# Range tests of the rounded weights: where they write, when they are issued, and where two roundings stand in their turns

## The chip, the core and the metric

The kernel runs on one core of one Trainium2 chip. The metric is the device time of one execution in microseconds (us). Before the change the median of three runs was 1049.61 us (1048.46 to 1050.42). The profiled execution had a span of 1047.8 us in the profile and 1049.67 us as a timed run.

A core has five engines that run their own instruction streams side by side: PE (matrix multiply), DVE (vector), ACT (activation functions), POOL (a second elementwise engine) and SP, which here only issues transfers. PEld stands for the weight loads of PE. Within one engine the instructions start in the order in which the program issues them.

## The reference, cut to what matters

```python
# q, k, v: (4, 8, 768, 64)   centroids: (8, 16, 64)
q_assign = argmax(q_n @ c_n), k_assign = argmax(k_n @ c_n)   # cluster of each row
scores = where(q_assign == k_assign, q @ k.T / 8, -1e9)
attn = softmax(scores);  y = attn @ v
x = y as (3072, 512)                      # (B*S, H*D)
h = x @ w_in                              # w_in (512, 2048)
out = (h * sigmoid(1.702 * h)) @ w_out    # w_out (2048, 512)
```

`w_in` and `w_out` arrive as 64-bit floats, which the kernel reads as pairs of 32-bit words and turns into 32-bit floats itself. That step is called rounding below.

## The kernel before, in words

`fast` does the whole computation under assumptions on the range of its data. It gathers evidence for these assumptions in a tile `row_sums`, and if a test at the end fails, a second function (`general`) computes everything again.

**Attention.** The 32 heads are handled as 16 pairs (`p`), four per batch. Queries are taken in halves of 384, so there are 32 groups `g` of one pair and one half, and each group has six units `u` (one tile of 128 keys each). The main loop (line 608) takes two units per **turn** `t`, with 96 turns and two more to drain. In a turn, in the order of issue: the scores of two units (PE, L397, and for the first four pairs a second product `part`, L411, that carries the cluster mask); their exponentials (ACT, L422); a weight rounding, if the table `pace` has one; the range test of the last softmax denominators (`check`, ACT, L481 and L483); the mask and the running sum (DVE L433 from turn 24 on, POOL L443); near scores of a later pair (`prep_near`, PE L289, copied by ACT L295); the values of the turn before (PE L454); every third turn a normalisation (PE L466, DVE reciprocal L469 and multiply L471); preparation of later pairs (transposes L275 with their copies L280 on ACT, cluster choice L300 to L321, one-hot copies L362 with L367 on DVE and L369 on ACT); chunks of the feed-forward part (PE L520 or L500, then ACT L490 and DVE L491); and a second rounding, in turns from 14 on.

Three PSUM banks named `m` serve the transposes, near scores, normalisation, feed-forward chunks and, in turns 5 to 13, the rounding. A PE instruction that needs a bank waits until the ACT or DVE instruction that reads the bank's previous content has ended.

**Rounding of the weights.** The weights are 32 chunks of 128x512 (0 to 15 are `w_in`, 16 to 31 `w_out`; chunk 31 is `w_out[:, 15, :]`). `load_w` fetches a chunk's pairs of words into one of three buffers `raw` (SP, 512 KB). `round_next(i)` takes chunk `i`: it issues the load of chunk `i + 2`, then four DVE operations (L177, L180, L182, L185; L177 and L180 read the high words, L185 the low words) and one addition L187, on DVE in turns 0 to 13 and on POOL from turn 14. Before the change chunks 0 to 7 belong to turns 0, 2, 5, 8, 9, 11, 12 and 13, and from turn 14 each turn has two: chunk 8 + 2(t - 14) in the middle (after the exponentials) and the next at the end. Turn 25 has chunks 30 and 31. In turn 13 the rounding stands at the end.

**Range test of a chunk.** `check_w` (L191) is two ACT operations, L197 (square) and L199 (exp), each with a sum along the row into `row_sums`. It is issued at the head of the *next* rounding, and it writes its elementwise result, which nobody uses, over the high words that it reads. So L197 waits until DVE's L180 of that chunk has read them. The load of chunk `i + 2` reuses the buffer of chunk `i - 1`, and so waits for L185 of that chunk and for its test.

`manual_schedule` keeps the order of issue as it is written. Before the change the test of chunk 0 stands in turn 2, that of chunk 1 in turn 5, that of chunk 31 in turn 26.

**After attention** (its last scores start at 587 us, the next product, L740, at 602 us) the rest of the feed-forward part follows, which the change does not touch.

Of the kernel before, what the change touches and what calls it, by code (L numbers as in the profile page):

```python
# [8 lines left out]
FP32 = mybir.dt.float32  # L9
# [4 lines left out]
AF = mybir.ActivationFunctionType  # L14
# [24 lines left out]
def fast(  # L39
# [26 lines left out]
    nc = tc.nc  # L66
# [11 lines left out]
    NF = DF // P  # L78
# [28 lines left out]
    def bank():  # L107
        return ps_m.tile([P, 512], FP32, name="m")
# [17 lines left out]
    def load_v(p):  # L126
# [16 lines left out]
    w_chunks = [  # L143
        (w[:, c, n:n + WN],
         src.bitcast(I32)[c * P:(c + 1) * P, 2 * n:2 * (n + WN)])
        for w, src, n_c, n_n in ((w_in, moe_w_in, NCH, DF),
                                 (w_out, moe_w_out, NF, DM))
        for n in range(0, n_n, WN) for c in range(n_c)]
    NW = len(w_chunks)
    w_raw, w_pow = {}, {}  # L150

    def load_w(i):
        if i < NW:
            t = wp.tile([P, WN, 2], I32, name="raw")
            nc.sync.dma_start(out=t.rearrange("p n t -> p (n t)"),
                              in_=w_chunks[i][1])
            w_raw[i] = t
# [2 lines left out]

    ODD = -2 ** 30
    POWER = -2 ** 23
    w_done, w_read = [0], {}

    def round_next(in_psum=False, engine=nc.gpsimd):

        i = w_done[0]
        if i - 1 in w_read:
            check_w(i - 1)
        if i == NW:  # L170
            return
        load_w(i + 2)
        raw, w = w_raw.pop(i), w_chunks[i][0]
        e = wp.tile([P, WN], I32, name="e", bufs=2)
        a = bank() if in_psum else w
        hi, lo, a_i = raw[:, :, 1], raw.bitcast(U32)[:, :, 0], a.bitcast(I32)
        nc.vector.tensor_scalar(out=a_i, in0=hi, scalar1=3, scalar2=0x3FFFFFF8,  # L177
                                op0=ALU.logical_shift_left,
                                op1=ALU.bitwise_and)
        nc.vector.scalar_tensor_tensor(out=a_i, in0=hi, scalar=ODD, in1=a_i,  # L180
                                       op0=ALU.bitwise_and, op1=ALU.bitwise_or)
        nc.vector.tensor_scalar(out=e, in0=a_i, scalar1=POWER, scalar2=None,  # L182
                                op0=ALU.bitwise_and)
        e = e.bitcast(FP32)
        nc.vector.scalar_tensor_tensor(out=e, in0=lo, scalar=2.0 ** -52, in1=e,  # L185
                                       op0=ALU.mult, op1=ALU.mult)
        engine.tensor_tensor(out=w, in0=a, in1=e, op=ALU.add)  # L187
        w_read[i] = raw
        w_done[0] += 1

    def check_w(i):  # L191

        y = w_read.pop(i).bitcast(FP32)[:, :, 1]
        nc.scalar.activation(out=y, in_=y, func=AF.Square,  # L197
                             accum_out=row_sums[:, 2, i:i + 1])
        nc.scalar.activation(out=y, in_=y, func=AF.Exp, scale=-2.0 ** 12,  # L199
                             bias=fifteen[:, 0:1],  # L200
                             accum_out=row_sums[:, 3, i:i + 1])

    def round_to(n):
        while w_done[0] < n:
            round_next()
# [51 lines left out]
    for a in range(2):  # L257
        rows = slice(a * D, (a + 1) * D)
        nc.vector.tensor_copy(
            out=cT[rows, :, a, :],  # L260
            in_=cps[rows, 0:P].rearrange("d (h a c) -> d h a c", a=2,
                                         c=NC)[:, :, a, :])
# [128 lines left out]
    def scores(u):  # L391
        g, kt = divmod(u, NJ)
        p, h = split(g)
        ps = ps_s.tile([P, 2, 512], FP32, name="s")
        for a in range(2):
            rows = slice(a * D, (a + 1) * D)
            nc.tensor.matmul(out=ps[:, a, 0:HALF],  # L397
                             lhsT=T[p, 1][rows, kt * P:(kt + 1) * P],
                             rhs=T[p, 0][rows, h * HALF:(h + 1) * HALF],
                             start=True, stop=(p >= HP))  # L400
        s_of[u] = ps[:, :, 0:HALF]

    def part(u):

        g, kt = divmod(u, NJ)
        p, h = split(g)
        if p >= HP:
            return
        for a in range(2):
            r = 32 * (2 * (p % 2) + a)  # L410
            nc.tensor.matmul(  # L411
                out=s_of[u][:, a, :],
                lhsT=hots[p // 2, 1][r:r + NC, kt * P:(kt + 1) * P],
                rhs=hots[p // 2, 0][r:r + NC, h * HALF:(h + 1) * HALF],
                start=False, stop=True)

    def exps(u):
        p, h = split(u // NJ)
        s = s_of[u]
        if p < HP:  # L420
            A_of[u] = ap.tile([P, 2, HALF], FP32, name="A")
        nc.scalar.activation(out=A_of[u] if p < HP else s, in_=s, func=AF.Exp,  # L422
                             scale=SCALE)

    def mask(u):

        g, kt = divmod(u, NJ)
        p, h = split(g)
        s = s_of.pop(u)
        if p >= HP:  # L430
            A_of[u] = ap.tile([P, 2, HALF], FP32, name="A")
            for a in range(2):
                nc.vector.scalar_tensor_tensor(  # L433
                    out=A_of[u][:, a, :],
                    in0=qcode[p][:, a, h * HALF:(h + 1) * HALF],
                    scalar=code[p][:, kt % NH, 1, kt // NH, a:a + 1],
                    in1=s[:, a, :], op0=ALU.is_equal, op1=ALU.mult)
        A = A_of[u]
        if kt == 0:
            return  # L440
        if kt == 1:
            sum_of[g] = ap.tile([P, 2, HALF], FP32, name="sum", bufs=2)
        nc.gpsimd.tensor_tensor(out=sum_of[g],  # L443
                                in0=A_of[u - 1] if kt == 1 else sum_of[g],
                                in1=A, op=ALU.add)
# [31 lines left out]
    def check(g):  # L477


        rec = recs.pop(g)  # L480
        nc.scalar.activation(out=rec, in_=rec, func=AF.Copy,  # L481
                             accum_out=row_sums[:, 0, g:g + 1])
        nc.scalar.activation(out=rec, in_=rec, func=AF.Relu, bias=top[:, 0:1],  # L483
                             scale=-2.0 * LIMIT * LIMIT,
                             accum_out=row_sums[:, 1, g:g + 1])
# [22 lines left out]
    half_ffn, ffn = deque(), deque()  # L508
# [63 lines left out]
    NT = NU // 2  # L572
    TG = NJ // 2
    TB = 2 * HP * TG

    prep_at = {}
    for p in range(1, NPAIR):
        b, hp = divmod(p, HP)
        for i in range(2 if p == 1 else 0, len(PREP)):
            if p == 1:  # L580
                t = (i - 2) // 2
            elif b == 0:
                t = (hp - 2) * TG + 1 + i // 2
            else:
                t = b * TB + TG * hp - (7, 7, 6, 6, 4, 3, 2)[i]
# [5 lines left out]
    def prep(p, i):  # L591
        if i == 0 and p:
            load_v(p)
        PREP[i](p)
        if i in (1, 3) and loads:
            load_qk(*loads.popleft())

    rate = 1.6


    pace = {t: 1 for t in (0, 2, 5, 8, 9, 11, 12, 13)}
    pace.update((t, 2) for t in range(TB // 2 + 2, NT))
    owed = 0.0
# [4 lines left out]
    for t in range(NT + 2):  # L608
        us = range(2 * t, 2 * t + 2) if t < NT else ()
        for u in us:  # L610
            scores(u)
        if t == 0:
            prep(0, 6)
        for u in us:
            part(u)
        for u in us:
            exps(u)
        second_half = t >= TB // 2
        how = ((False, nc.gpsimd) if t >= TB // 2 + 2 else
               (t > 2, nc.vector))  # L620
        if pace.get(t) and t != TB // 2 + 1:
            round_next(*how)
        if recs:
            check(*recs)
        for u in us:
            mask(u)
        work = sorted(prep_at.get(t, ()), key=lambda w: PREP[w[1]] != prep_near)
        while work and PREP[work[0][1]] == prep_near:
            prep(*work.pop(0))
        if 1 <= t <= NT:  # L630
            for u in range(2 * t - 2, 2 * t):
                values(u)

        kept = NF // 2 if t < NT - 3 else NF // 4
        todo = half_ffn or (ffn if len(ffn) > kept else ())
        owed += (rate if half_ffn else 0.65 if kept > NF // 4 else 1.0) if todo else -owed
        g = (t - 2) // TG if t >= 2 and (t - 2) % TG == TG - 1 else None
        if g is not None and second_half:
            normalise(g)
        for p, i in work:  # L640
            prep(p, i)
        if g is not None and not second_half:
            normalise(g)
        while owed >= 1 and todo:
            todo.popleft()()
            owed -= 1
        if pace.get(t) == 2 or t == TB // 2 + 1:
            round_next(*how)
    check(*recs)
    qcode.clear()  # L650
# [649 lines left out]
```

## Time and profile before

| what | value |
|---|---|
| median of three runs | 1049.61 us |
| span of the profiled execution | 1047.8 us |
| PE busy, 0 to 228 us / 228 to 1048 us | 192.2 us / 804.9 us |
| DVE busy, 88 to 148 us | 55.2 us of 60 |
| idle of ACT before L197, ended by DVE's L180 | 20.8 us in 11 waits |
| load of one weight chunk, issue to landing (min, median, max) | 3.5, 4.0, 6.0 us |

The page of a profile gives busy times and a strip of 40 slices, each with a digit for its busy share in tenths. The row PEclk in that strip is the clock that PE was granted. The answers on waits give the engine and line that stood idle, the engine and line whose end released it, and total us, number and longest. A row of the timeline has the start, the duration, the engine, the line, the operation and its tiles, and in brackets the idle time of that engine just before and its releaser. The rounding and its tests lie in the first 220 us. All turns up to 26 lie there: turn 2's exponentials start at 25.68, turn 3's at 37.06, turn 14's at 88.15, turn 20's at 144.03, turn 21's at 161.85, turn 25's at 205.47 and turn 26's at 216.27.

### The profile page before, as it was taken

To read this page: it belongs to the slowest core of one execution; us is meant where nothing else is said; L and a number is where in the kernel's file an instruction comes from. 1 tells how busy PE (TensorE), PEld (TensorE's weight loads), DVE (VectorE), ACT (ScalarE), POOL (GpSimd) and SP (SyncE) were. 2 spreads that over 40 slices of the span, in tenths; PEclk is the share of its full clock that TensorE was granted. 3 is DMA by queue.
4 is the path that set the end of the run, shared out by engine and by line. 5 is a ranking of instruction groups with operands and counts; after the bars stand their busy time and mean duration, and the time that the engine had idled before them with its cause. 6 is when DMAs were issued, how large, how long until landed. Compare 5 with 4: busy or idle time off the path is not lost.

```text
span 1047.8 us, 12571 instructions
## 1 busy us (share of the span) xinstructions
PE 997.1 (95%) x4574; PEld 583.0 (56%) x4574; DVE 677.4 (65%) x1055; ACT 374.2 (36%) x761; POOL 418.8 (40%) x304
## 2 busy tenths in 40 slices
PE   7799778889999999999999999999999999999997
PEld 3334334334455345544455355688755788655886
DVE  4679887764577867776877577743477634576431
ACT  4567554642355545555554322200022200222000
POOL 2565654443466556655666767600022100120000
PEclk9999888999999999999999999999999999999999
DMA  7323443520002310131000000000000000000000
GB/s 219 79 71 119 132 146 96 153 63 18 19 17 61 91 39 19 31 83 40 26 1 1 1 11 0 1 21 21 21 0 1 1 21 21 21 0 1 21 21 23
DMA packets 66118, 45.25 MB, mean 43 GB/s; under 512 B 52096, under 2 KB 60032, under 8 KB 66048
## 3 DMA queue, kind: packets, MB, share of 16 engines
q1 hardware_dynamic: 65904, 44.33, 14.7%
q8 instruction: 38, 0.62, 0.2%
q14 instruction: 32, 0.26, 0.1%
q10 hardware_dynamic: 144, 0.03, 0.0%
HBM read 38.04 MB, written 6.31 MB: 42 GB/s over the span
## 4 chain that ended last, share of the span: by engine, by line
PE 83%; DVE 10%; ACT 4%; issue 1%; DMA 0%; POOL 0%; SPq 0%; DVEq 0%; ACTq 0%; POOLq 0%
PE b L797 21%; PE b L740 21%; PE s L397 11%; PE o L454 10%; PE m L500 7%; PE m L549 4%; PE m L520 3%; PE m L275 2%; PE m L466 2%; DVE short L469 1%; DVE e L185 1%; DVE w_in L180 1%; PE m L289 1%; DVE w_out L180 1%; DVE A L433 1%
## 5 line engine op out<-in xcount | busy, mean ns | idle before, releaser
L443 POOL TENSOR_TENSOR sum<-sum,A 128x768 f32<-128x768 f32 x128 | 235.2, 1837 | 135.0 <-DVE A L433 114.3
L433 DVE SCALAR_TENSOR_TENSOR A<-qb,code,s 128x384 f32<-128x384 uint8 x288 | 157.4, 607 | 86.3 <-ACT s L422 51.3
L397 PE MATMUL s<-T,T 64*128 64x384 f32 x768 | 155.6, 519 | 2.5 <-DVE A L433 0.6
L454 PE MATMUL o<-A,inv 128*64 128x384 f32 x768 | 146.0, 502 | 1.1 <-ACT x L459 1.1
L422 ACT ACTIVATE s<-s 128x768 f32<-128x768 f32 x144 | 108.8, 793 | 103.1 <-PE s L397 90.8
L731 DVE TENSOR_TENSOR G<-b,G 128x384 f32<-128x384 f32 x168 | 93.3, 555 | 48.5 <-PE b L740 41.6
L678 POOL TENSOR_TENSOR W<-w_in 128x256 f32<-128x256 f32 x24 | 17.7, 738 | 261.2 <-PE b L740 259.4
L490 ACT ACTIVATE th<-G 128x384 f32<-128x384 f32 x96 | 50.2, 523 | 163.5 <-DVE G L731 103.1
L397 PEld LDWEIGHTS s<-T,T 64*128 64x128 f32 x768 | 66.1, 188 | 76.0 <-issue 35.0
L731 DVE TENSOR_TENSOR y<-b,y 128x256 f32<-128x256 f32 x54 | 22.1, 422 | 130.1 <-PE b L797 93.8
L740 PE MATMUL b<-x,w_in 128*128 128x384 f32 x288 | 101.2, 486 | 0.0
L454 PEld LDWEIGHTS o<-A,inv 128*64 128x64 f32 x768 | 46.9, 137 | 86.3 <-issue 82.5
L469 DVE RECIPROCAL short<-m 128x384 f32<-128x384 f32 x32 | 81.6, 2551 | 7.3 <-PE m L466 7.1
L443 POOL TENSOR_TENSOR sum<-A 128x768 f32<-128x768 f32 x32 | 58.4, 1826 | 67.4 <-DVE A L433 32.3
L491 DVE SCALAR_TENSOR_TENSOR G<-th,G 128x384 f32<-128x384 f32 x96 | 68.5, 713 | 16.8 <-ACT th L490 14.2
L740 PEld LDWEIGHTS b<-x,w_in 128*128 128x128 f32 x288 | 54.7, 190 | 37.9 <-issue 0.5
L740 PE MATMUL b<-x,W 128*128 128x384 f32 x192 | 71.0, 493 | 0.0
L797 PE MATMUL b<-Z,G 128*128 128x256 f32 x288 | 65.1, 379 | 0.0
L797 PE MATMUL b<-w_out,G 128*128 128x256 f32 x288 | 63.6, 379 | 0.0
L520 PE MATMUL m<-x,w_in 128*128 128x384 f32 x128 | 50.7, 552 | 11.8 <-ACT short L295 6.8
L500 PE MATMUL m<-w_out,g 128*128 128x512 f32 x120 | 59.1, 611 | 2.3 <-ACT T L280 2.3
L797 PEld LDWEIGHTS b<-w_out,G 128*128 128x128 f32 x288 | 54.6, 190 | 8.0
(122 smaller groups left out, 1339.2 us busy)
## 6 DMA issues: line engine op xcount, KB each, us to landing
raw<-in_moe_w_in_dram SPq DMA_DIRECT2D x16, 512.0 KB, 4.2
raw<-in_moe_w_out_dram SPq DMA_DIRECT2D x16, 512.0 KB, 3.5
in<-in_q_dram SPq DMA_DIRECT2D x32, 192.0 KB, 4.2
in<-in_k_dram SPq DMA_DIRECT2D x32, 192.0 KB, 3.2
inv<-in_v_dram SPq DMA_DIRECT2D x16, 384.0 KB, 4.0
out_dram<-y SPq DMA_DIRECT2D x15, 256.0 KB, 2.4
qb<-line SPq DMA_DIRECT2D x12, 192.0 KB, 3.3
out_dram<-y SPq DMA_DIRECT2D x18, 128.0 KB, 1.8
```

What stands on the lines that cost most here:

```text
L397: nc.tensor.matmul(out=ps[:, a, 0:HALF], lhsT=T[p, 1][rows, kt * P:(kt + 1) * P], rhs=T[p, 0][rows, h * HALF:(h + 1) * HALF], start=True, ...
L422: nc.scalar.activation(out=A_of[u] if p < HP else s, in_=s, func=AF.Exp, scale=SCALE)
L433: nc.vector.scalar_tensor_tensor(out=A_of[u][:, a, :], in0=qcode[p][:, a, h * HALF:(h + 1) * HALF], scalar=code[p][:, kt % NH, 1, kt // NH ...
L443: nc.gpsimd.tensor_tensor(out=sum_of[g], in0=A_of[u - 1] if kt == 1 else sum_of[g], in1=A, op=ALU.add)
L454: nc.tensor.matmul(out=o_of[g][a * D:(a + 1) * D, 0:HALF], lhsT=v_in[p][:, a, kt, :], rhs=A[:, a, :], start=(kt == 0), stop=(kt == NJ - 1))
L469: nc.vector.reciprocal(out=rec, in_=ps[:, 0:HALF])
L491: nc.vector.scalar_tensor_tensor(out=g, in0=t, scalar=1.0, in1=h, op0=ALU.add, op1=ALU.mult)
L500: nc.tensor.matmul(out=ps[:, 0:DM], lhsT=g, rhs=w_out[:, f, :], start=(f == 0), stop=(f == NF - 1))
L520: nc.tensor.matmul(out=ps[:, 0:HALF], lhsT=w_in[:, c, f * P:(f + 1) * P], rhs=xT[c], start=(c == 0), stop=(c == NCH - 1))
L731: nc.vector.tensor_tensor(out=o, in0=p, in1=a, op=ALU.add)
L740: nc.tensor.matmul(out=ps[:, 0:HALF], lhsT=a[:, c], rhs=x(c), start=(c == 0), stop=(c == 1))
L797: nc.tensor.matmul(out=ps[:, 0:DN], lhsT=a(f // 4)[:, f % 4], rhs=z(f), start=(f == 0), stop=(f == FB - 1))
```

## The change

Four things change. The test of chunk `i` is issued right after the rounding of the same chunk, where before it stood ahead of the next one. Its elementwise result goes to the place of chunk 31 in `w_out`, which is empty until chunk 31 itself is rounded; only the test of chunk 31 still writes over its own high words. The roundings of turns 0 and 2 are issued at the end of their turns. And the line that counts feed-forward chunks (`owed`) is written out in branches with the same values.

```diff
     def round_next(in_psum=False, engine=nc.gpsimd):
         i = w_done[0]
-        if i - 1 in w_read:
-            check_w(i - 1)
         if i == NW:
             return
         load_w(i + 2)
...
         engine.tensor_tensor(out=w, in0=a, in1=e, op=ALU.add)
-        w_read[i] = raw
+        check_w(i, raw, w_chunks[NW - 1][0] if i < NW - 1 else raw.bitcast(
+            FP32)[:, :, 1])
         w_done[0] += 1
-    def check_w(i):
-        y = w_read.pop(i).bitcast(FP32)[:, :, 1]
-        nc.scalar.activation(out=y, in_=y, func=AF.Square,
+    def check_w(i, raw, z):
+        nc.scalar.activation(out=z, in_=raw.bitcast(FP32)[:, :, 1],
+                             func=AF.Square,
                              accum_out=row_sums[:, 2, i:i + 1])
-        nc.scalar.activation(out=y, in_=y, func=AF.Exp, scale=-2.0 ** 12,
+        nc.scalar.activation(out=z, in_=z, func=AF.Exp, scale=-2.0 ** 12,
                              bias=fifteen[:, 0:1],
                              accum_out=row_sums[:, 3, i:i + 1])
...
-        if pace.get(t) and t != TB // 2 + 1:
+        late = t <= 2 or t == TB // 2 + 1
+        if pace.get(t) and not late:
             round_next(*how)
...
-        if pace.get(t) == 2 or t == TB // 2 + 1:
+        if pace.get(t) == 2 or pace.get(t) and late:
             round_next(*how)
```

No instruction is added or removed on any engine. In the built program the order on DVE differs in one place (in turn 2, L367 comes ahead of the rounding of chunk 1), on ACT each test stands one place earlier (that of chunk 31 at the end of turn 25), and on SP the loads of chunks 2 and 3 come after a pair of q loads.

More of the change, by code (lines that the diff above doesn't have):

```diff
@@ L162, in fast @@
     POWER = -2 ** 23
-    w_done, w_read = [0], {}
+    w_done = [0]
     def round_next(in_psum=False, engine=nc.gpsimd):
         i = w_done[0]
-        if i - 1 in w_read:
-            check_w(i - 1)
         if i == NW:
@@ L635, in fast @@
         todo = half_ffn or (ffn if len(ffn) > kept else ())
-        owed += (rate if half_ffn else 0.65 if kept > NF // 4 else 1.0) if todo else -owed
+        if not todo:
+            owed = 0.0
+        elif half_ffn:
+            owed += rate
+        else:
+            owed += 0.65 if t < NT - 3 else 1.0
         g = (t - 2) // TG if t >= 2 and (t - 2) % TG == TG - 1 else None
```

## The prediction

> **What bounds the kernel now.** I first read the page's busy times and clock strip, to see where PE, the busiest engine, loses time.
>
> ```profile
> PE 997.1 (95%) x4574; PEld 583.0 (56%) x4574; DVE 677.4 (65%) x1055; ACT 374.2 (36%) x761; POOL 418.8 (40%) x304
> PEclk9999888999999999999999999999999999999999
> ```
>
> PE lacks 50.7 us of the span. By windows, 35.8 of them lie before 228 us (192.2 busy), and there the clock drops too. The change touches nothing later, so only this stretch can gain, and from 228 us on PE is full (40.00 of 40 us in 248 to 288), so what is won or lost before should reach the end one to one. Next come the waits, which name what PE and ACT stood still for.
>
> ```profile
> PE m L520 <- ACT short L295: 6.8, 2, 5.0
> PE m L275 <- DVE qb L367: 4.7, 1, 4.7
> PE m L275 <- ACT short L295: 2.7, 1, 2.7
> ACT raw L197 <- DVE w_in L180: 12.1, 6, 4.4
> ACT raw L197 <- DVE w_out L180: 7.4, 4, 3.9
> ACT raw L197 <- DVE m L180: 1.3, 1, 1.3
> ```
>
> The last three are the 20.8 us in which ACT waits for a rounding to read its words. Whether they cost anything depends on what stands behind them, so I read the timeline at the three long waits of PE: in turn 2,
>
> ```profile
> 26.77 2.24 DVE L180 SCALAR_TENSOR_TENSOR w_in<-raw,w_in 128x512 int32<-128x512 int32 x1
> 29.05 1.91 DVE L182 TENSOR_SCALAR e<-w_in 128x512 int32<-128x512 int32 x1
> 32.44 0.56 DVE L367 COPY qb<-m 64x768 bf16<-64x768 bf16 x1
> 33.06 0.61 PE L275 MATMUL m<-ident,in 128*128 128x128 f32 x3 [4.73 <-DVE qb L367]
> ```
>
> in turns 20 and 21,
>
> ```profile
> 149.39 0.67 ACT L197 ACTIVATE raw<-raw 128x512 f32<-128x512 f32 x1 [3.87 <-DVE w_out L180]
> 152.69 7.19 PE L520 MATMUL m<-x,w_in 128*128 128x384 f32 x16 [4.96 <-ACT short L295]
> 155.18 3.70 POOL L443 TENSOR_TENSOR sum<-sum,A 128x768 f32<-128x768 f32 x2
> 167.81 5.46 PE L520 MATMUL m<-x,w_in 128*128 128x384 f32 x8 [3.43 <-DVE short L309]
> ```
>
> and in turns 25 and 26.
>
> ```profile
> 216.27 1.50 ACT L422 ACTIVATE s<-s 128x768 f32<-128x768 f32 x2 [3.44 <-PE s L397]
> 218.18 0.69 DVE L180 SCALAR_TENSOR_TENSOR w_out<-raw,w_out 128x512 int32<-128x512 int32 x1
> 218.91 0.69 ACT L197 ACTIVATE raw<-raw 128x512 f32<-128x512 f32 x1 [1.15 <-DVE w_out L180]
> 221.72 0.46 ACT L295 COPY short<-m 128x384 f32<-128x384 f32 x1
> 222.23 0.55 PE L275 MATMUL m<-ident,in 128*128 128x128 f32 x3 [2.67 <-ACT short L295]
> ```
>
> The reader should see: in turn 2 a whole rounding of 6.1 us stands ahead of a 0.56 us copy that PE needs; in turn 20 ACT's wait for DVE is passed on to PE through L295; in turn 25 the last chunk's L180 ends only at 218.87, after the exponentials of turn 26 have begun.
>
> **What the skill says.** (1) "TensorE: Matmul & The Clock Gate", Part 1: PE's clock is halved after an idle window of about 3.4 us and restored after a busy one, and the windows run free of the program. The trace agrees: after the 4.96 us wait sixteen L520 take 7.19 us, where sixteen elsewhere take 5.43, with a clock of 0.50 in 150 to 156 us; but idle times from 2.1 us (at 52 us) already halved it, and one of 2.67 us did not. (2) "SBUF — State Buffer", section Who interferes with whom: a DVE instruction with two inputs in SBUF, or in a two-port mode, and a GpSimd (POOL) instruction that reads SBUF exclude each other for the whole instruction. The trace agrees: L180 takes 0.69 us alone and 2.24 beside POOL's sums. (3) The same TensorE page, section on the 32x32 array: ACT and DVE are strict first in, first out. So a test that waits holds everything behind it; L295 at 152.18 shows it.
>
> **The change, part by part.**
>
> *Turn 2: the rounding of chunk 1 moves behind L367 (DVE), its L197/L199 to the end of the turn (ACT), the load of chunk 3 behind two q loads (SP).* The one-hot transposes start at 27.02; at 43.01 the same copy starts 0.53 us after them, so L367 would run at 27.55 to 28.11. PE's first three transposes end at 28.34, so the 4.73 us wait goes to nothing. The scores behind it took 2.93 us at the halved clock, against 1.56 usually: 1.4 more. On ACT, L369 no longer stands behind the test of chunk 0, so the copies L280 end about 29.6; then comes chunk 1's test, 1.65 us, and the exponentials of turn 3 at 31.25 where PE would allow 30.95. Before they start at 37.06: **gain 5.8**. Bounds: 6.1 without the test in the way; 4.3 if the moved rounding, which now meets POOL's sums of both turns, holds up L306 of turn 3 (free until 34.05 by my count, rounding done about 33.1) by one sum less its margin, 1.5. I take 5.8. Chunk 3's load isn't needed before turn 8; SP gives its place to q loads that wait for PE.
>
> *Turn 0: the same move.* On DVE no other instruction changes places with it. On ACT the test of chunk 0 falls into 18.25 to 19.9, inside the 2.10 us that ACT idles before 20.34. The load of chunk 2 goes from 14.52 to about 18.6, needed at 48.87. Nothing, hidden by those.
>
> *Turns 14 to 19: waits of L197.* Seven of the eleven waits lie here, 13.4 us. DVE is 55.2 us busy of 60 in 88 to 148, and PE waits for it (L469, L491), not for ACT. ACT would run ahead of DVE and wait for loads instead: a load now follows L185 of the chunk three before, plus 4.0 us; chunk 14's would land about 114.4 where ACT comes by about 112.4. Where PE gains 0.4 us (turn 17), the DVE work behind it then waits for POOL's L443. Nothing, hidden by DVE; at most 1.
>
> *Turn 20.* Chunk 20's load lands about 144, so its test starts at 145.5, when the exponentials end, instead of 149.39. From L197 to L295 it is 2.79 us, so L295 starts at 148.3 and L520 at 148.8: 3.9 earlier, and with 1.1 us idle the clock stays up (1.76). PE ends sixteen L520 at 154.3, 5.6 earlier. But the next rounding on DVE then falls from 155.4 into POOL's L443 (155.18 to 158.88). Its two last operations (0.43 and 0.69) come after that: done at about 160.4, before at 163.31. The next rounding and L306, L309 follow unbroken, and L520 of turn 21 waits for L309: 165.0 instead of 167.81. **Gain 2.8**; bounds 0 and 5.6 (no loss to POOL, or all of it).
>
> *Turns 25 and 26: the test of chunk 31.* It is the one that still writes over its words, and now stands at the end of turn 25, ahead of the exponentials of turn 26. A wait is added: ACT is held from about 209.7 until L180 ends at 218.87. Behind it: both L422 of turn 26, L481, L483, L295, L280; for these wait DVE's masks, and PE's L275. The test takes 1.57, so the exponentials start at 220.5 instead of 216.27. The test no longer stands behind them, so L295 starts at 223.2 instead of 221.72: 1.5 later. PE then idles 4.2 us instead of 2.67, which by the cases above should halve the clock for one window, 1.7 of work. **Loss 3.2**; bounds 1.5 (clock stays up) and 4.9 (two windows, as in 115 to 122 us).
>
> Sum: -5.8 - 2.8 + 3.2 = **-5.4** on the span of 1047.8. That execution was timed at 1049.67, beside a median of 1049.61, so I take the median: **1044.2 us**.
>
> **The rivals.** (a) *POOL takes all of turn 20's gain*: -5.8 + 3.2 = -2.6, 1047.0. For it: DVE is the bound there, and three of the four rounding operations have been seen stretched to about 2 us; against it: DVE idles 3.98 and 2.03 us in that stretch. (b) *The last test costs nothing*, as DVE comes to it earlier or PE finds other work: -8.6, 1041.0. For it: PE has two matmul groups ready (L454, L397); against it: they end before 219.6. (c) *The waits are only replaced*: in turn 2 L369 or a load takes L367's place and ACT waits for loads elsewhere, so the change doesn't do what it says: 1049.6. Against it: L369 would end at 28.7, long before 33. (d) *Slower: the held ACT queue of turn 25.* If all 10.8 us from 209.7 to 220.5 came onto the path instead of their tail, the sum would be -8.6 + 10.8 = +2.2: 1051.8. It decides from 8.6. Against it: before, too, ACT starts nothing of turn 26 until 216.27, as PE's scores come only then.
>
> **How the numbers follow.** Forecast 0.50, (a) 0.20, (b) 0.18, (c) 0.06, (d) 0.06. About 0.2%, 2.1 us, is what a measurement of this kernel can tell from no change, so faster means below 1047.5. Case (a) lies 0.5 us inside that; I give it 0.14 of faster and 0.06 of same. Faster 0.50 + 0.18 + 0.14 = 0.82, same 0.06 + 0.06 = 0.12, slower 0.06. The range goes down past (b) by the open 1.5 of turns 2 and 20, to 1039.5, and up past (a) by 1.0 of clock windows, to 1048.0; (c) and (d), 0.12, stay out.
>
> **What would show it.** Right: PE's wait for L367 gone and turn 3's exponentials 5 to 6 us earlier; no L197 released by L180 except one, of about 9 us, before turn 26; PE's wait for L295 near 149 down to about 1 us; a longer one for L309 near 159 (5 to 6 us) and for L295 near 215 (about 4 us). Wrong: L197 waits for loads by many us, or PE's wait near 215 grows with the whole hold.

## The result, and the profile after

The changed kernel takes 1042.84 us (median of four runs, 1041.59 to 1044.41), beside 1049.03 us for the kernel before: ratio 0.9941, 95% interval 0.9922 to 0.9959. Run again beside other kernels (7 below) it took 1042.45 us (1041.06 to 1042.99), ratio 0.9915 (0.9892 to 0.9937). It is faster: by 6.2 us in the first comparison and by 10.0 in the second, where the kernel before had a median of 1052.42 us. The prediction was a gain of 5.4 us, to 1044.2. The profiled execution has a span of 1040.6 us, where the one of before had 1047.8. From here on, lines 196 and 199 are the range test that stood at L197 and L199; the rounding is now L175, L178, L180, L183 and L185.

The page of the changed kernel, busy times and clock strip:

```profile
PE 993.8 (96%) x4574; PEld 583.8 (56%) x4574; DVE 681.7 (66%) x1055; ACT 372.8 (36%) x761; POOL 418.6 (40%) x304
PEclk9999898999999999999999999999999999999999
```

PE lacks 46.8 us of the span, against 50.7 before. Half of the 7.2 us, then, is idle time that is gone; the rest is PE busy time, 997.1 to 993.8: the same matmuls at a higher clock. What PE waited for in the first 230 us, and what ACT waited for before the tests (line, releaser, total us, number, longest):

```profile
PE m L520 <- DVE short L309: 5.2, 1, 5.2
PE m L275 <- ACT short L295: 4.1, 1, 4.1
PE m L520 <- DVE x L491: 2.8, 2, 2.1
PE m L520 <- ACT short L295: 2.4, 2, 1.7
```

```profile
ACT raw L196 <- DVE w_out L178: 10.3, 1, 10.3
...
ACT w_out L196 <- DMA raw<-in_moe_w_in_dram: 6.7, 3, 2.6
```

The 4.7 us for L367 are gone from PE's list. The 6.8 us for L295 before L520 are 2.4. Three waits have grown: L309 from 3.4 to 5.2, L295 before L275 from 2.7 to 4.1, and L491 before L520 from 1.1 to 2.8 (its longest from 0.6 to 2.1, in turn 16). On ACT the eleven waits for the rounding are one, of 10.3 us; three waits for loads have come in their place.

Where the time went is read by laying the starts of ACT's exponentials (L422) of chosen turns side by side. "Again" is the profile of the changed kernel's second measurement.

| stretch | before, us | changed | again | predicted difference | measured, changed / again |
|---|---|---|---|---|---|
| start to turn 2 | 25.68 | 25.30 | 26.04 | 0 | -0.4 / +0.4 |
| turn 2 to 3 | 11.38 | 5.32 | 5.30 | -5.8 | -6.1 / -6.1 |
| turn 3 to 7 | 23.06 | 21.12 | 22.67 | 0 | -1.9 / -0.4 |
| turn 7 to 14 | 28.03 | 28.18 | 28.19 | 0 | +0.2 / +0.2 |
| turn 14 to 20 | 55.88 | 56.33 | 57.53 | 0, at most 1 | +0.5 / +1.7 |
| turn 20 to 22 | 31.23 | 28.87 | 27.33 | -2.8 | -2.4 / -3.9 |
| turn 22 to 25 | 30.21 | 30.00 | 29.98 | 0 | -0.2 / -0.2 |
| turn 25 to 27 | 21.64 | 24.81 | 24.61 | +3.2 | +3.2 / +3.0 |
| turn 27 to the end | 820.7 | 820.7 | 819.1 | 0 | 0 / -1.6 |
| span | 1047.8 | 1040.6 | 1040.7 | -5.4 | -7.2 / -7.1 |

Two executions of the same kernel agree on the span, and differ by 1.2 to 1.6 us in four of the stretches. That is the clock, as shown below.

Turn 2 in the timeline of the changed kernel (start, duration, engine, line, in brackets the idle time before):

```profile
27.17 0.56 DVE L367 COPY qb<-m 64x768 bf16<-64x768 bf16 x1 [1.15 <-PE m L362]
...
28.38 2.19 DVE L178 SCALAR_TENSOR_TENSOR w_in<-raw,w_in 128x512 int32<-128x512 int32 x1
29.08 0.69 ACT L196 ACTIVATE w_out<-raw 128x512 f32<-128x512 f32 x1
...
30.62 1.49 ACT L422 ACTIVATE A<-s 128x768 f32<-128x768 f32 x2
```

The copy now runs ahead of the rounding. The rounding's slow operation, stretched to 2.19 us beside POOL's sum, lies behind it and holds nobody. The test starts at 29.08, though its own L178 runs until 30.57: it writes into `w_out` and follows its load alone.

Turns 20 and 21:

```profile
141.59 7.12 PE L520 MATMUL m<-x,w_in 128*128 128x384 f32 x16 [0.74 <-ACT short L295]
...
150.44 2.19 DVE L178 SCALAR_TENSOR_TENSOR w_out<-raw,w_out 128x512 int32<-128x512 int32 x1
...
157.65 0.56 DVE L309 TENSOR_TENSOR short<-m,best 128x384 bf16<-128x384 f32 x1
...
158.36 4.83 PE L520 MATMUL m<-x,w_in 128*128 128x384 f32 x8 [5.16 <-DVE short L309]
```

PE's wait just ahead of turn 20's L520 is 0.74 us, where it was 4.96. The wait that follows, for DVE's L309 in turn 21, is longer instead.

Turns 25 and 26:

```profile
207.90 0.69 DVE L178 SCALAR_TENSOR_TENSOR w_out<-raw,w_out 128x512 int32<-128x512 int32 x1
208.63 0.69 ACT L196 ACTIVATE raw<-raw 128x512 f32<-128x512 f32 x1 [10.34 <-DVE w_out L178]
...
210.18 1.48 ACT L422 ACTIVATE s<-s 128x768 f32<-128x768 f32 x2
...
212.84 0.46 ACT L295 COPY short<-m 128x384 f32<-128x384 f32 x1
...
213.35 0.70 PE L275 MATMUL m<-ident,in 128*128 128x128 f32 x3 [4.14 <-ACT short L295]
213.85 1.92 PE L500 MATMUL m<-w_out,g 128*128 128x512 f32 x2
```

ACT stands 10.34 us before the last test, with the exponentials of turn 26 behind it. PE stands 4.14 us, and L500 then runs at half clock: 1.92 us, where 1.02 is usual.

### The profile page after: what moved, and what is told of

Read it like the earlier page. It is cut to its first block, busy times and chain, and to the rows that moved or that the text cites. A ratio compares the mean times of both kernels' runs of the same rounds, so it can differ in the third digit from the quotient of the medians.

```text
span 1040.6 us, 12560 instructions
## 1 busy us (share of the span) xinstructions
PE 993.8 (96%) x4574; PEld 583.8 (56%) x4574; DVE 681.7 (66%) x1055; ACT 372.8 (36%) x761; POOL 418.6 (40%) x304
## 4 chain that ended last, share of the span: by engine, by line
PE 83%; DVE 13%; ACT 2%; issue 1%; DMA 0%; POOL 0%; DVEq 0%; ACTq 0%
PE b L803 21%; PE b L746 21%; PE s L397 11%; PE o L454 10%; PE m L500 7%; PE m L549 4%; PE m L520 3%; PE m L275 2%; DVE short L469 2%; DVE e L183 2%; PE m L466 2%; DVE w_out L178 1%; DVE e L180 1%; DVE A L433 1%; DVE w_in L178 1%
## 5 line engine op out<-in xcount | busy, mean ns | idle before, releaser
L454 PE MATMUL o<-A,inv 128*64 128x384 f32 x768 | 145.1, 499 | 1.0 <-ACT x L459 1.0
L422 ACT ACTIVATE s<-s 128x768 f32<-128x768 f32 x144 | 109.0, 793 | 99.5 <-PE s L397 87.1
L454 PEld LDWEIGHTS o<-A,inv 128*64 128x64 f32 x768 | 46.6, 136 | 85.1 <-issue 81.4
L491 DVE SCALAR_TENSOR_TENSOR G<-th,G 128x384 f32<-128x384 f32 x96 | 68.6, 714 | 16.8 <-ACT th L490 14.2
L500 PE MATMUL m<-w_out,g 128*128 128x512 f32 x120 | 60.0, 619 | 2.2 <-ACT T L280 2.2
L520 PE MATMUL m<-x,w_in 128*128 128x384 f32 x128 | 49.3, 542 | 10.3 <-DVE short L309 5.2
```

Of the source, the lines that this page charges most:

```text
L454: nc.tensor.matmul(out=o_of[g][a * D:(a + 1) * D, 0:HALF], lhsT=v_in[p][:, a, kt, :], rhs=A[:, a, :], start=(kt == 0), stop=(kt == NJ - 1))
L491: nc.vector.scalar_tensor_tensor(out=g, in0=t, scalar=1.0, in1=h, op0=ALU.add, op1=ALU.mult)
L500: nc.tensor.matmul(out=ps[:, 0:DM], lhsT=g, rhs=w_out[:, f, :], start=(f == 0), stop=(f == NF - 1))
L520: nc.tensor.matmul(out=ps[:, 0:HALF], lhsT=w_in[:, c, f * P:(f + 1) * P], rhs=xT[c], start=(c == 0), stop=(c == NCH - 1))
```

## The experiments

Two sets of four kernels, each set on one chip. The median of before was 1050.91 us (1048.12 to 1054.23, 19 runs) beside the first set and 1052.42 us (1047.86 to 1054.40, 11 runs) beside the second. The ratios are to before. Its runs spread over 6.1 and 6.5 us, with granted clocks from 0.979 to 0.984, and its one profiled execution (timed at 1049.67 us) lies in the faster half of both sets. So the differences of medians come out larger here than those between the profiles; what the slower runs of before lose, and where, no trace here shows.

| kernel | median, us (range) | ratio, 95% interval | profiled span, us |
|---|---|---|---|
| 1 the move alone | 1041.37 (1040.54 to 1042.43) | 0.9902, 0.9883 to 0.9921 | 1040.6 |
| 2 the tests alone | 1050.86 (1048.81 to 1051.59) | 0.9991, 0.9978 to 1.0003 | 1049.1 |
| 3 last test in a tile of its own | 1035.16 (1034.19 to 1035.50) | 0.9844, 0.9826 to 0.9863 | 1032.4 |
| 4 last test later | 1039.53 (1039.01 to 1042.50) | 0.9893, 0.9874 to 0.9912 | 1037.6 |
| 5 no POOL sum in turn 20 | 1040.81 (one run) | none | 1039.0 |
| 6 as 3, turn 21's rounding late | 1033.48 (1031.11 to 1034.22) | 0.9828, 0.9803 to 0.9854 | 1031.6 |
| 7 the changed kernel again | 1042.45 (1041.06 to 1042.99) | 0.9915, 0.9892 to 0.9937 | 1040.7 |
| 8 kernel 3 again | 1036.15 (1035.31 to 1037.30) | 0.9857, 0.9832 to 0.9881 | 1035.4 |

### 1 and 2: the two halves of the change

Kernel 1 is the kernel before with only the roundings moved; kernel 2 is the changed kernel with only that undone.

```diff
# 1, from the kernel before
-        if pace.get(t) and t != TB // 2 + 1:
+        late = t <= 2 or t == TB // 2 + 1
+        if pace.get(t) and not late:
...
-        if pace.get(t) == 2 or t == TB // 2 + 1:
+        if pace.get(t) == 2 or pace.get(t) and late:
# 2, from the changed kernel
-        late = t <= 2 or t == TB // 2 + 1
+        late = t == TB // 2 + 1
```

> The kernel before with one part of the change: the roundings of turns 0 and 2 stand at the end of their turns; every range test stays where it was before. My theory: the whole gain of turn 2 is this move. The exponentials of turn 3 start about 6.1 us earlier than before, counted from those of turn 2, and the time is 5 to 7.5 us below the kernel before (about 6, ratio 0.994; 1.6 us either way hang on whether a clock window of PE falls into the wait of turn 5). Rival: the tests carry the gain, and the move alone gives under 2 us.

> The changed kernel with the roundings of turns 0 and 2 back in the middle of their turns; the tests follow the loads as in the change. My theory: turns 14 to 22 give 2 to 3 us, the last test takes 3.2 back, so the time is within 2 us of the kernel before (ratio 0.999 to 1.001), with a wait of about 10 us of ACT before the last test. Rival: the tests carry the gain, and this version alone is 4 us or more faster.

In kernel 1 turn 2 to 3 took 5.37 us, 6.0 less than before; turn 20 to 22 took 31.88, no less than before's 31.23; turn 25 to 27 took 20.40, without the loss. (Turn 3 to 7 is 1.9 shorter here too, and 22 to 25 1.7 longer.) PE's waits in 138 to 178 us still show before's wait for L295 in full:

```profile
PE m L520 <- ACT short L295: 4.9, 1, 4.9
PE m L520 <- DVE short L309: 3.4, 1, 3.4
```

Kernel 2, timeline of turn 2:

```profile
32.22 0.56 DVE L367 COPY qb<-m 64x768 bf16<-64x768 bf16 x1
...
32.84 0.90 PE L275 MATMUL m<-ident,in 128*128 128x128 f32 x3 [4.72 <-DVE qb L367]
```

From turn 7 on its stretches are those of the changed kernel: turn 20 to 22 28.88 us (-2.4), turn 25 to 27 24.81 (+3.2).

So the move alone gives the gain of the whole change: kernel 1 and the changed kernel have the same profiled span, and the interval of its ratio overlaps that of kernel 7 (they did not run side by side). Kernel 1's median is 9.5 us below that of before, more than the 5 to 7.5 expected, while its span is 7.2 below: the profiled execution of before was 1.2 us faster than the median there, and that of kernel 1 1.1 slower. The tests by themselves can't be told from no change, because their gain in turn 20 is spent again in turn 25, along with the small losses of turns 3 to 20 (+0.8 together).

### 3 and 4: the last test

```diff
# 3, from the changed kernel
-        check_w(i, raw, w_chunks[NW - 1][0] if i < NW - 1 else raw.bitcast(
-            FP32)[:, :, 1])
+        check_w(i, raw, w_chunks[NW - 1][0] if i < NW - 1 else yp.tile(
+            [P, DM], FP32, name="y"))
# 4, from the changed kernel: chunk 31's test, in place, in the middle of turn 26
...
+        if i < NW - 1:
+            check_w(i, raw, w_chunks[NW - 1][0])
+        else:
+            w_read[i] = raw
...
```

> The changed kernel, but the test of chunk 31 writes its elementwise result into the output tile y, which nothing uses before turn 26, so it too follows its load alone. My theory: ACT's wait of 10.3 us before the last test goes, the exponentials of turn 26 start 4.2 us earlier, PE's wait for L295 near 213 falls from 4.1 us to under 0.5 and its clock stays up: 4 to 6 us below the changed kernel, about 1037.5. Rival: the wait is hidden by other work and the version is within 1 us of the changed kernel.

> The changed kernel, but the test of chunk 31 stands where it stood before the change, in the middle of turn 26, and writes over its own words. My theory: the exponentials of turn 26 start 4.2 us earlier than in the changed kernel, but the test then stands behind them and holds L295: PE waits about 2.7 us as before the change, with its clock up. About 3 us below the changed kernel, near 1040, between the changed kernel and the version with the free last test. Rival: the place of the last test does not matter, within 1 us of the changed kernel.

Kernel 3, timeline around turns 25 and 26:

```profile
197.29 0.68 ACT L196 ACTIVATE y<-raw 128x512 f32<-128x512 f32 x1
...
205.00 1.50 ACT L422 ACTIVATE s<-s 128x768 f32<-128x768 f32 x2 [6.09 <-PE s L397]
...
206.99 0.69 DVE L178 SCALAR_TENSOR_TENSOR w_out<-raw,w_out 128x512 int32<-128x512 int32 x1
```

The test of chunk 31 runs 9.7 us ahead of the L178 that it used to wait for, and the exponentials of turn 26 wait for PE's scores alone. Turn 25 to 27 takes 19.10 us: 5.7 less than in the changed kernel, and 2.5 less than before. Kernel 4 (its lines stand 5 further down: L427 exponentials, L201 test, L300 copy, L280 transposes):

```profile
206.07 1.50 ACT L427 ACTIVATE s<-s 128x768 f32<-128x768 f32 x2 [7.62 <-PE s L402]
...
208.77 0.69 ACT L201 ACTIVATE raw<-raw 128x512 f32<-128x512 f32 x1 [1.21 <-DVE w_out L181]
...
212.09 0.55 PE L280 MATMUL m<-ident,in 128*128 128x128 f32 x3 [2.73 <-ACT short L300]
```

Turn 25 to 27 takes 21.69 us there, as before (21.64), with before's wait of 2.7 us. The place of this one test is thus worth 3.1 us. Freed, at the end of turn 25, it gains another 2.6; no run splits these between the wait (1.21 us) and the test's own length (about 1.5 us), which both stand ahead of L295 in kernel 4. Kernel 3 is faster than the kernels before and after the change: 6.3 us below the changed kernel beside which it was run (8 against 7), where 4 to 6 were expected at first. It is also 6.2 us below kernel 1, so the tests, once the last one is freed too, are worth that much on top of the move.

### 5: does POOL's sum take the rest of turn 20's gain?

The kernel leaves the units of turn 20 (40 and 41) out of POOL's running sum, so that two terms are missing from it.

```diff
-        if kt == 0:
+        if kt == 0 or u in (40, 41):
```

> The changed kernel without POOL's running sum (L443) of the two units of turn 20, so two terms are missing from that sum. It asks whether this sum is what takes the rest of turn 20's gain: in the changed kernel the next rounding's L178 takes 2.19 us beside it at 150.44 and PE waits 5.16 us for L309 near 158.4. If POOL's sum is the cause, that L178 takes about 0.7 us, L309 ends 1.5 to 2 us earlier against turn 20's exponentials, PE's wait for it falls to about 3.5 us, and turn 22's exponentials start about 27.0 us after turn 20's instead of 28.9. Rival: DVE's own queue is the cause whatever POOL does; then the distance stays within 0.5 us of 28.9.

```profile
149.73 0.69 DVE L178 SCALAR_TENSOR_TENSOR w_out<-raw,w_out 128x512 int32<-128x512 int32 x1
...
155.46 0.56 DVE L309 TENSOR_TENSOR short<-m,best 128x384 bf16<-128x384 f32 x1
...
156.16 5.46 PE L520 MATMUL m<-x,w_in 128*128 128x384 f32 x8 [3.42 <-DVE short L309]
```

L178 takes 0.69 us, and the wait for L309 is 3.42. The execution to compare it with is kernel 7, in which, as here, turn 20's L520 ran at full clock. There POOL's sum stretches two operations of the rounding (L175 to 2.08 us from 0.42, L178 to 2.20 from 0.69, 3.2 together), and the wait is 6.58: 3.2 longer. In the changed kernel's first profile L178 alone is stretched by much, and the wait is 5.16: 1.7 longer. So POOL's sum is what lengthens this wait. Turn 20 to 22 takes 25.56 us, 1.8 less than kernel 7's 27.33 (1.9 was expected, counted from the changed kernel); the rest of the 3.2 went to the clock, since turn 21's eight L520 took 5.46 us here and 4.22 there. Nor did the 1.8 last: in turn 24 the same wait of 1.71 us for L280 cost half clock here (two and six L500 in 1.88 and 3.73 us, against 1.13 and 2.74 in kernel 7), which took 1.7 back.

### 6: one rounding fewer ahead of L309

```diff
# from kernel 3
-        late = t <= 2 or t == TB // 2 + 1
+        late = t <= 2 or t in (TB // 2 + 1, 21)
...
-        if pace.get(t) == 2 or pace.get(t) and late:
+        for _ in range(pace.get(t, 0) - (not late)):
             round_next(*how)
```

> The kernel with the last test in a tile of its own, and with both roundings of turn 21 at that turn's end. In that kernel PE waits 6.3 us for L309, which stands on DVE behind the rounding in the middle of turn 21. Theory (the wait is for a DVE queue with one rounding too many ahead of L309): the wait falls to about 3 us, turn 22's exponentials start 3 to 4 us earlier, and the time is 3 to 5 us below that of the kernel without this edit (about 1031 to 1032 where that one gives 1035). Rival (DVE bounds turns 20 to 25 as a whole): the two roundings in a row hold the masks and copies of turn 22, the gain is given back by turn 25, and the time is within 1 us of the kernel without this edit.

```profile
155.85 2.85 PE L520 MATMUL m<-x,w_in 128*128 128x384 f32 x8 [0.24 <-ACT T L280]
156.20 0.55 DVE L306 TENSOR_REDUCE best<-m 128x24 f32<-128x384 f32 x1
156.78 0.56 DVE L309 TENSOR_TENSOR short<-m,best 128x384 bf16<-128x384 f32 x1
```

L306 starts 17.61 us after turn 20's exponentials, against 20.84 in kernel 8: 3.2 sooner, the length of one rounding, as expected. But PE's wait went from 5.14 us to 0.24, by more than that, and L520 starts before L309 at all. The built program tells why. In kernel 3 this L520 writes the bank `m` that L309 reads; in kernel 6 the pool of these banks gave it the bank of the first transposes L275, which ACT's L280 frees. So the wait for DVE is gone altogether, and the 3.2 us alone would have left about the 3 us expected. Against kernel 8 (both with turn 20's L520 at 7.12 us) turn 20 to 22 takes 23.72 instead of 28.85 us, in part by the clock (turn 21's eight L520 in 2.85 us instead of 4.80); turn 25 to 27 gives 1.6 back, and 3.9 remain by turn 28. The medians differ by 2.7, a little under the 3 to 5 expected; the spans by 3.8. Kernel 6 is the fastest of all, 9.0 us below the changed kernel on that chip.

### 7 and 8: the same kernels again

> The changed kernel as it is, beside the others on one chip, so that they can be compared with it. It should repeat its time of about 1042.8 us, ratio 0.994 to the kernel before, and its steps: turn 3's exponentials at about 30.6 us, 28.9 us from turn 20's exponentials to turn 22's, 24.8 from turn 25's to turn 27's. If the 1.6 us between turns 6 and 7 is a matter of where a clock window falls, it may be missing here; if it is part of the change, it is there again.

> The kernel with the last test in a tile of its own, again, beside the other three. It should give about 1035 us, 6 to 8 below the changed kernel on the same chip: 5.7 from turns 25 to 27 and, if the 1.6 us near 590 us is more than chance, that too. If that was a clock window that fell well by chance, the difference may be near 6.

Kernel 8 stands 6.3 us below kernel 7, within the expected 6 to 8. Kernel 7 repeats the time, but not the ratio, since the kernel before was slower beside it. It repeats the steps of turns 2 and 25, but not those of turns 3 to 7, of 14 to 22 and of the end. Turns 5 and 6, the changed kernel and then kernel 7:

```profile
47.11 0.85 PE L289 MATMUL m<-T,cT 128*32 128x384 f32 x8 [2.08 <-DVE w_in L185]
47.89 1.51 PE L454 MATMUL o<-A,inv 128*64 128x384 f32 x8
```

```profile
47.85 1.50 PE L289 MATMUL m<-T,cT 128*32 128x384 f32 x8 [2.08 <-DVE w_in L185]
49.28 2.39 PE L454 MATMUL o<-A,inv 128*64 128x384 f32 x8
```

After attention, in the same order:

```profile
599.49 1.65 PE L746 MATMUL b<-T,W 128*128 128x384 f32 x2 [2.55 <-DVE T L684]
600.93 2.35 PE L746 MATMUL b<-x,W 128*128 128x384 f32 x4
```

```profile
601.24 0.91 PE L746 MATMUL b<-T,W 128*128 128x384 f32 x2 [2.55 <-DVE T L684]
601.99 1.45 PE L746 MATMUL b<-x,W 128*128 128x384 f32 x4
```

The same wait, to the hundredth, is followed by full clock in one execution and by half clock in the other: 1.5 to 1.6 us each time. In the kernel before both fell badly (L289 1.51, L454 2.48, and 809.2 us from turn 28 to the end, as in the changed kernel; 807.6 in kernel 7). So the 1.6 us between turns 6 and 7 belong to no part of the change. Nor do those after attention that kernel 3 seemed to have gained: kernels 6, 7 and 8 have them too.

## Why the prediction was right, step by step

**Turn 2, -5.8 predicted, -6.1 measured.** The copy L367 was placed at 27.55 us; with the 0.38 us by which the changed kernel reached turn 2 sooner, it started at 27.55. The test began 0.1 sooner than expected and took 1.5 us instead of 1.65. Kernels 1 and 2 show that this step is the move alone.

**Turn 0 and turns 14 to 19, 0 predicted, or at most 1.** Turn 0 is below what the start tells: two executions lie 0.4 on either side. In turns 14 to 19 ACT did turn from waiting for DVE to waiting for loads, as written (6.7 us in three waits). That DVE hides the gain is true of the sum: in the changed kernel turns 14 and 15 are 2.4 us shorter than before, and turns 16 and 17 give 2.9 back. In turn 16 PE now waits 2.1 us for DVE's L491, where before had 0.52 and kernel 1 0.55. The stretch grew by 0.3 and 0.5 us in kernel 2 and the changed kernel, and by 1.7 in kernel 7, which is beyond the bound of 1. That excess is the clock. After nearly the same wait the changed kernel and then kernel 7 show

```profile
99.06 2.85 PE L520 MATMUL m<-x,w_in 128*128 128x384 f32 x8 [2.13 <-DVE x L491]
```

```profile
101.29 4.54 PE L520 MATMUL m<-x,w_in 128*128 128x384 f32 x8 [2.09 <-DVE x L491]
```

and kernel 7's granted clock is 0.50 from 102.29 to 105.71 us. Kernels 3 and 5 have this drop too. In these three turn 20's L520 then ran at full clock, so most of it came back there. Turn 14 to 22 together is 1.9 us shorter than before in the changed kernel and 2.2 in kernel 7.

**Turn 20, -2.8 predicted, -2.4 and -3.9 measured.** The chain was right: L295 no longer waits for a test, counted from the exponentials L520 starts 3.3 to 4.0 us sooner (3.9 expected), and the next rounding falls into POOL's sum, which kernel 5 prices. What I had wrong is that the clock "stays up" once the wait is 1.1 us. In the changed kernel sixteen L520 took 7.12 us behind waits of 0.29, 1.00 and 0.74, in kernel 7 5.43 behind 0.40 and 1.03. Which of the two happens depends on how the waits fall into the clock's windows (last section), and it is worth 1.5 by turn 22. So the size was right in part by luck: counted from turn 20's exponentials, L520 of turn 21 starts 1.7 us sooner than before in the changed kernel and 2.6 in kernel 7 (2.8 in the working), and the rest is its own clock (4.83 and 4.22 us for eight, where before took 5.46). Rival (a), that POOL takes all, is refuted: these 1.7 and 2.6 us are left with its sum in place.

**Turns 25 and 26, +3.2 predicted, +3.2 and +3.0 measured.** L178 of chunk 31 ended 13.47 us after turn 25's exponentials (13.40 in the working), turn 26's started at 15.06 (15.03), PE waited 4.14 us (4.2), and the two groups of L500 behind it took 1.6 us more (1.7). Rival (b), that the last test costs nothing, and rival (d), that its whole hold comes onto the path, both fall: ACT was held 10.3 us and the end moved by 3.2. Kernels 3 and 4 show that the loss takes both the place and the wait: kernel 3 keeps the place, kernel 4 keeps a wait of 1.21 us, and neither has the loss.

**The sum.** -5.4 became -7.2 in the profiled span. Turns 3 to 7, at which nothing was predicted, hold -1.9 of it, 1.6 of that the clock of turns 5 and 6; the other deviations cancel to 0.1. In kernel 7 the same total came from other windows. A sum of waits could not have told these apart in advance. The medians moved by 6.2 us in the first comparison and by 10.0 in the second, and most of that difference lies in the kernel before (3.4 us slower there), for a cause that stays open. So it is luck, too, that the first came within 1 us of the forecast. Rival (c), that waits are only replaced, falls for the whole change, but is true of the tests taken by themselves (kernel 2, ratio 0.9991), and for a reason that it did not name: not loads, but the one test left in place.

## What to carry to other kernels

A wait of an in-order engine costs what the instructions behind it cost; the same kind of test was worth 2.4 us in one turn, nothing in seven waits, and -3.2 in another. When a dependence is removed from all instances of an operation but one, look at that one first: moved forward with the others it stands in a worse place, and giving it a tile of its own was worth another 6.3 us. If a bank comes from a pool, moving its reader can also change which bank the next writer gets, so the list of waits in the built program is to be read again after each move.

## What was not expected of the hardware

The Trainium skill, "TensorE: Matmul & The Clock Gate", Part 1, speaks of free-running activity windows of about 3.4 us. That the windows run free agrees with these runs: identical waits of 1.71, 2.08 and 2.55 us were followed by half clock in one execution and full clock in another. Their length agrees too: apart from the start and the end of each execution, every stretch of half clock in the ten traces lasts 3.41 or 6.83 us, and those of one trace start whole multiples of 3.41 us apart.

What differs is how much idle time it takes: about half a window was enough, not a whole one. In kernel 7 the wait of 2.08 us in turn 6 put 1.91 us of idle time into the window from 44.27 to 47.68 us, and the next window ran at half clock. In the changed kernel a boundary at 46.37 cut the same wait into 1.34 and 0.74, and the clock stayed up. In turn 20 three short waits, none over 1.0 us, put 1.96 us into one window of the changed kernel (138.53 to 141.94), and half clock followed (7.12 us for sixteen L520); in kernel 7 the waits of 0.40 and 1.03 fell into two windows, and it did not (5.43). With the windows of all ten traces laid out in this way (20 to 1000 us), none that ran at full clock with less than 1.7 us of PE idle was followed by half clock, and none with more than 1.95 by full clock; from 1.7 to 1.95 both occur.

Each window at half clock costs 1.5 to 1.7 us here, so two executions of one kernel can agree on the span to 0.1 us and still differ by that much stretch by stretch. A gain of that size in one profile has to be seen in a second before it is believed.
